# Block sums made in PSUM, a new order of block products and other pages for copies, in the middle stage of an attention and mixture-of-experts kernel

## The chip, the cores and the metric

The kernel runs on one core of a Trainium2 chip. The metric is the device time of one execution in microseconds (us). The engines are TensorE (PE, matmuls), VectorE (DVE), ScalarE (ACT), GpSimd (POOL), and SyncE (SP), whose queue issues most of the DMAs.

## The reference

`x` is the output of an attention block (a local window plus a downsampled part), 2304 tokens by 512. All numbers are fp32. Behind it stands a layer of eight experts, and it is there that the change lies:

```
P = exp(logits - logits.max())          # then normalised eight times by rows and columns
out = np.zeros((N, D), dtype=np.float32)
for e in range(E):                      # E = 8, D = 512, F = 1024
    h = np.maximum(x @ w1[e], 0.0)
    ye = h @ w2[e]
    out += P[:, e:e + 1] * ye
```

## The kernel before, in words

**Precision.** Every fp32 operand of a matmul is split into a high part (fp32r, made by ACT with a copy) and a low part (the rest, made by DVE or POOL with a subtraction). A product takes three matmuls: high by high, high by low, low by high.

**Stages.** The attention and the first experts come first (up to about 668 us). In the *middle stage* (class `Mid`, `final_plan(form="X")`, 668 to 914 us) three experts are computed for 1024 tokens by a fast block product: seven products of blocks instead of eight, for the price of sums of blocks before and after. A short *plain part* (`plain_part`, L2599 on, 914 to 953 us) follows: eight steps of ordinary products (`mm1` L2312, `mm2` L2331 to L2333), during which the operands of the last stage are prepared. The *last stage* (class `Final`, form "Y") does all eight experts for the last 1024 tokens, again with seven products, and keeps PE busy to the end.

**A round of the middle stage.** There are six rounds s (three experts, two halves of F each). A round has first-layer products `a1`..`a7` and `b1`..`b7` (the letter is the half of the columns of F) and second-layer products `1`..`7` that use the round before. A first-layer product is 6 matmuls of 512 columns (L573), a second-layer product 4 tiles of 6 matmuls of 256 columns (L755). The order on PE is written out by hand in strings: `PROX` for the first round, `MIDX` for the five next ones, `TAILX` for what is left of the second layer at the end.

The first-layer products go to two PSUM banks of a side, A (products 1, 6, 7, 4, summed in this order) and D (2, 5, 3). Between them ACT copies the bank to SBUF (`s1` after 1, `u2` after 6, `u3` after 7), and DVE forms sums: `c11` after 2, `c22` after 5 and 7, `c12` after 3. `c11` starts as bank D plus `s1`, and the bank is then started anew by product 5. When all seven are there, four more sums of relus are made (`S1` to `S4`). The function `hl` splits each result: `hi` on ACT, `lo` on DVE. The sums c11, c21, S1, S2, S3, S4, c12 are the operands of products 2, 1, 5, 6, 7, 3, 4 of the second layer. The results of the second layer are multiplied by the gate and added to accumulators by DVE (L766).

**Who sets the order.** `Plan.schedule` gives each operation a due time, counted back from PE's order, and writes every engine's queue in an order that follows from it. Pages of SBUF come from pools; `Mid.make` (L689 on) says which ring of values lies where: `five` are the eight pages of tile x5, `wb` and `ct` are pools with 8 and 4 pages. `self.five[6]` and `[7]` are free for sums or copies because the weights of layer one use six.

**Around the end of the middle stage.** The operands x4 and x5 of the last stage had been stored to `xc` in DRAM. `reload` (L2790) brings back two of the four slices of four tiles: the first half is issued behind the last first-layer product, the second half behind everything. `soon` (L2798) starts the weights of the plain part. In `plain_part`, `next(tg)` draws five operations at a time (`per`) from `t_gen` (L2620 on): sums of blocks of x4 and x5 (`bsum`, DVE L2627), split into `th` (ACT L2644) and `tl` (DVE). Their four buffers in pool `ct` are then taken by the gates `g` of the last stage (DMA L562).

Of the kernel before, what the change touches and what calls it, by code (L numbers as in the profile page):

```python
# [8 lines left out]
F32 = mybir.dt.float32  # L9
# [157 lines left out]

PRO = "a1 a2 f a6 a5 f b1 b2 a7 f f a4 f a3 b6 f b5 b7 f b4 b3 f".split()
MID = "1 a1 a2 2 a6 a5 5 a7 b1 6 a4 a3 3 b2 b6 7 b5 b7 4 b4 b3".split()
MIDX = "2 a1 a2 1 a6 a5 5 a7 b1 6 a4 a3 3 b2 b6 7 b5 b7 4 b4 b3".split()  # L170
PROX = "a1 a2 f a6 a5 f b1 b2 a7 f f a4 f a3 b6 f b5 b7 f b4 b3 f".split()
TAILX = "2 1 6 5 7 3 4".split()
MIDL = "1 a1 a2 2 a6 a5 5 a7 b1 6 a4 b2 3 a3 b6 b5 b7 7 b4 b3 4".split()
TAIL = "1 2 5 6 x11 7 3 x22 4 x12 4 x21".split()

# [1 line left out]
def final_plan(  # L177
# [3 lines left out]
    P = Plan()  # L181

    def E(f, *a):
        return lambda: getattr(em, f)(*a)
# [63 lines left out]
    def l1(s, p, i, conv, st):  # L248
        k = f"{p}{s}"
# [20 lines left out]
        if form == "X":  # L270
            if i == 2:
                m = st["m11"] = new(f"m11{p}")
                P.dve(f"c11 {k}", [bk, st["s1"]], [m], E("add", m, bk, st["s1"]))
                hl("c11", m, True, False, True)
            if i in (5, 7) and 5 in st and 7 in st:
                m = st["m22"] = new(f"m22{p}")
                P.dve(f"c22 {k}", [st[5], st["u3"]], [m], E("add", m, st[5], st["u3"]))
                P.act(f"r22 {k}", [m], [m], E("relu", m, m))
            if i == 3:
                P.dve(f"c12 {k}", [bk, st["u2"]], [bk], E("add", bk, bk, st["u2"]))  # L280
                hl("c12", bk, False, True, True)
            if i == 4:
                hl("c21", bk, False, True, True)
            if all(z in st for z in range(1, 8)):
                A, D, m11, m22, ms = st[4], st[3], st["m11"], st["m22"], new("ms")
                P.dve(f"S1 {k}", [D, m22], [ms], E("rcomb", ms, D, m22, False))
                P.dve(f"S3 {k}", [A, m22], [m22], E("rcomb", m22, A, m22, True))
                P.dve(f"S2 {k}", [A, ms], [A], E("rcomb", A, A, ms, True))
                hl("S1", ms, True, False)
                hl("S2", A, False, True)  # L290
                hl("S3", m22, True, False)
                P.dve(f"S4 {k}", [m11, A], [m11], E("rcomb", m11, m11, A, False))
                hl("S4", m11, True, False)
            return
        if i == 2:
            m = st["m11"] = new("m11" if masters == 2 else f"m11{p}")
# [351 lines left out]
class Mid(Final):  # L648
# [25 lines left out]
        self.first_r2 = 5 * len(es) * 2 % 6  # L674

    def page(self, home, z, dt=F32R):
        k = z in ("h", 0)
        if home in ("wa", "wb"):
            return self.take(home, "w1h" if k else "w1l", dt, "hx")
        if home == "hp":  # L680
            return self.take("hp", "hh" if k else "hl", dt, "hx")
        if home == "ct":
            return self.take("ct", "s", dt, "hx")
        if home == "four":
            return self.four[7]
        return self.rest.pop(0)

    def make(self, ring, i):
        if ring == "o1":  # L689
            t = self.four[i].rearrange("p (a c) -> p a c", a=4)  # L690
            return {"h": t[:, 0:2], "l": t[:, 2:4]}
        if ring == "o2":
            return {z: self.take("wa", "w2" + z, F32R, "o2").rearrange("p (a c) -> p a c", a=2) for z in "hl"}
        if ring in ("r1", "m11b", "m22b"):
            if not self.five:
                for z in "hl":
                    t = self.xq.tile([128, 4, 512], F32, name=f"x{z}5")
                    self.five += [t[:, k] for k in range(4)]
            return self.five[{"m11b": 6, "m22b": 7}.get(ring, i)]
        if ring == "r2":  # L700
            for n in (0, 3, 5, 4, 2, 1):
                self.made["r2", (self.first_r2 + n) % 6] = self.take("rawp", "r", F32, "r2")
            return self.made[ring, i]
        if ring == "ms":
            return self.take("ct", "s", F32, ring)
        if ring in ("s13", "u2", "m11a", "m22a"):
            return self.page("wb", int(ring in ("u2", "m22a")), F32)
        if ring[0] == "h":
            x, p = ring[1:-1], ring[-1]
            return {z: self.page(self.home[x, p, z], z) for z in "hl"}  # L710
        pool, tag = {"A": ("ps_h", "h"), "D": ("ps_a", "a"), "Y": ("ps_y", "y"), "Z": ("ps_z", "y")}[ring[0]]
        return self.take(pool, tag, F32, "psm")
# [62 lines left out]
def attention_moe_kernel(  # L775
# [1577 lines left out]
    with tc.manual_schedule():  # L2353
# [189 lines left out]
        new = []  # L2543
# [164 lines left out]
        def plain_part(rest, n0, limit, tg, ahead, held, h_next=None):  # L2708

            steps = [(p, e, f, n0 + i * NF + f) for i, (p, e) in enumerate(rest) for f in range(NF)]  # L2710
            per = -(-24 // max(1, len(steps) - 3))
            for si, (piece, e, f, n) in enumerate(steps):
                h_cur = mm1(piece, n) if h_next is None else h_next
                if si == 0:
                    while part1:
                        plain2()
                h_next = mm1(steps[si + 1][0], steps[si + 1][3]) if si + 1 < len(steps) else None
                if f == 0:
                    ye = [y_tile([128, DM], "psy") for _ in piece_tiles(piece)]
                pump(clk["pe"], clk["pe"] - 0.15)  # L2720
                if si >= len(steps) - 2:
                    held.append((
                        lambda t, h=h_cur, n=n, f=f, y=ye: mm2(h, n, y[t:t + 1], f, t),
                        lambda t, e=e, y=ye, l=piece_tiles(piece): combine(*l[t], e, y[t], accp),
                    ))
                else:
                    t2 = mm2(h_cur, n, ye, f)
                if f == NF - 1 and si < len(steps) - 2:
                    for (c, t), y in zip(piece_tiles(piece), ye):
                        combine(c, t, e, y, accp)  # L2730
                        dve(512, t2)
                while n_cv[0] < min(n + 5, limit):
                    w_convert(nc.vector)
                for _ in range(per if si >= 2 else 0):
                    next(tg, None)
                pump(clk["pe"], clk["pe"] - 0.15)
                ahead(si - len(steps))
# [59 lines left out]
        def soon():  # L2797
            for _ in range(2 * NRAW - 1):  # L2798
                raw_next()
            for _ in plain1():  # L2800
                pass

        then = {
            id([o for o in plan.seq if o.name == f"2t0 {ns - 1}"][0]): raw_next,
            id([o for o in plan.seq if o.name[0] in "ab"][-1]): lambda: reload(slice(0, 4, 2)),
            id([o for o in work if o.name.startswith("w2l")][-1]): soon,
        }
        for o in work:
            if o not in first:
                o.emit()  # L2810
            then.get(id(o), lambda: None)()
        reload(slice(1, 4, 2))
        for c, t in closing:
            closed(c, t, accp)
        final = Final(
# [58 lines left out]
```

## Time and profile before

| | us |
|---|---|
| median of 3 runs (1593.80 to 1597.13) | 1594.59 |
| the profiled execution: time | 1595.28 |
| the profiled execution: span on the core | 1593.5 |
| PE busy | 1569.8 (99%) |
| DVE busy | 1364.5 (86%) |
| POOL busy | 1080.3 (68%) |
| ACT busy | 810.7 (51%) |

The span runs from the first instruction to the last; 1.78 us of the execution lie around it. PE is busy nearly all the time, so what can be had are its idle stretches and those in which its clock is lower. These stand at the end of the slices 24 and 25 of 40 (956 to 1012 us), which are the end of the plain part and the beginning of the last stage; there are small ones in the middle stage.

### The profile page before, as it was taken

What the parts mean: (1) busy time and instruction counts of PE and PEld (TensorE: products, weight loads), DVE (VectorE), ACT (ScalarE), POOL (GpSimd) and SP (SyncE); (2) the same over time, 40 slices, a digit from 0 to 9 for tenths busy, and PEclk for the clock granted to TensorE, in tenths of its full rate; (3) what the DMA queues carried; (4) which work ended last, traced back from release to release, by engine and by line L of the source; (5) the groups of instructions that cost most, each with busy time, mean ns of one, the idle gap of its engine ahead of it and who ended that gap; (6) DMA issues with size and microseconds to landing.
All of it is one profiled execution on the core that took longest, in us unless ns stands there. A gap on an engine that the chain in (4) does not pass through costs nothing.

```text
span 1593.5 us, 24471 instructions
## 1 busy us (share of the span) xinstructions
PE 1569.8 (99%) x8220; PEld 1324.4 (83%) x8220; DVE 1364.5 (86%) x1878; ACT 810.7 (51%) x1739; POOL 1080.3 (68%) x998
## 2 busy tenths in 40 slices
PE   9999999999999999999999997999999999999998
PEld 7888888888888888888988986788888888888887
DVE  8678998778988587389999867899999999999987
ACT  4554555565455443354555344555555555555553
POOL 6688656868585500378888557777777777777772
PEclk9999999999999999999999998999999999999999
DMA  7878766868584645423331363222221222222101
GB/s 201 214 204 210 168 171 176 209 179 225 147 222 117 182 150 169 140 75 90 111 99 48 118 207 80 65 62 65 61 67 56 74 57 69 66 77 55 47 14 53
DMA packets 230701, 191.23 MB, mean 120 GB/s; under 512 B 26479, under 2 KB 188463, under 8 KB 230575
## 3 DMA queue, kind: packets, MB, share of 16 engines
q1 hardware_dynamic: 223470, 177.87, 41.2%
q10 hardware_dynamic: 7104, 11.80, 2.0%
q8 instruction: 64, 1.05, 0.3%
q14 instruction: 63, 0.51, 0.1%
HBM read 167.42 MB, written 22.18 MB: 119 GB/s over the span
## 4 chain that ended last, share of the span: by engine, by line
PE 83%; DVE 7%; DMA 3%; POOL 3%; issue 2%; ACT 1%; SPq 1%; ACTq 0%; POOLq 0%; DVEq 0%
PE psm L573 22%; PE psm L586 19%; PE psh L2072 17%; PE psy L2106 6%; PE psy L2107 5%; PE psy L2108 5%; PE psm L755 4%; DVE acc L766 2%; DVE acc L2597 1%; DVE hx L733 1%; POOL o L556 1%; PE pss L1697 1%; DMA r<-in_moe_w_dram 1%; DMA xl<-xc 1%; PE psg L1877 1%
## 5 line engine op out<-in xcount | busy, mean ns | idle before, releaser
L556 POOL TENSOR_TENSOR o<-r,o 128x512 fp32r<-128x512 f32 x126 | 169.2, 1343 | 68.9 <-ACT o L552 66.5
L2228 POOL TENSOR_TENSOR w1l<-r,w1h 128x512 fp32r<-128x512 f32 x112 | 156.6, 1398 | 85.0 <-ACT w1h L2205 78.0
L573 PE MATMUL psm<-th,o 128*128 128x512 f32 x512 | 174.6, 392 | 7.0 <-DVE s L602 4.7
L2228 POOL TENSOR_TENSOR w2l<-r,w2h 128x512 fp32r<-128x512 f32 x114 | 159.3, 1397 | 28.7 <-ACT w2h L2205 28.4
L2106 PE MATMUL psy<-w2h,hh 128*128 128x512 f32 x408 | 166.0, 407 | 0.0
L2107 PE MATMUL psy<-w2l,hh 128*128 128x512 f32 x408 | 159.9, 392 | 0.0
L2108 PE MATMUL psy<-w2h,hl 128*128 128x512 f32 x408 | 159.8, 392 | 0.0
L586 PE MATMUL psm<-hx,o 128*128 128x512 f32 (+1 forms) x588 | 155.2, 387 | 0.0
L556 POOL TENSOR_TENSOR o<-xh,o 128x256 fp32r<-128x256 f32 x132 | 110.9, 842 | 62.5 <-ACT o L552 61.9
L596 DVE TENSOR_TENSOR acc<-psm,acc 128x512 f32<-128x512 f32 x214 | 143.1, 679 | 7.7 <-PE psm L586 7.5
L2136 ACT ACTIVATE hh<-psh 128x512 fp32r<-128x512 f32 (+1 forms) x136 | 67.5, 496 | 161.0 <-PE psh L2072 151.5
L2139 DVE SCALAR_TENSOR_TENSOR hl<-psh,hh 128x512 fp32r<-128x512 f32 (+1 forms) x136 | 76.2, 560 | 76.4 <-ACT hh L2136 76.2
L573 PE MATMUL psm<-xh,o 128*128 128x512 f32 x384 | 132.0, 392 | 2.9 <-DVE hx L611 1.9
L2205 ACT ACTIVATE w2h<-r 128x512 fp32r<-128x512 f32 x133 | 83.7, 629 | 90.4 <-PE psy L2108 27.6
L586 PEld LDWEIGHTS psm<-hx,o 128*128 128x128 f32 x588 | 109.4, 189 | 22.2
L2072 PE MATMUL psh<-xhs,w1h 128*128 128x256 f32 (+1 forms) x384 | 125.1, 326 | 0.3 <-ACT xhs L1838 0.3
L2072 PE MATMUL psh<-xhs,w1l 128*128 128x256 f32 (+1 forms) x384 | 122.9, 320 | 1.2 <-DVE w1l L2224 1.2
L2072 PE MATMUL psh<-xls,w1h 128*128 128x256 f32 (+1 forms) x384 | 122.8, 320 | 0.2
L573 PEld LDWEIGHTS psm<-th,o 128*128 128x128 f32 x512 | 96.7, 189 | 28.2 <-DVE s L602 5.2
L556 POOL TENSOR_TENSOR xh<-xh,xh 128x256 fp32r<-128x256 f32 x32 | 27.5, 867 | 123.2 <-ACT xh L552 123.1
L1283 DVE TENSOR_REDUCE lo<-prod 128x256 f32<-128x1792 f32 x32 | 109.5, 3422 | 0.4
L552 ACT ACTIVATE o<-r 128x512 fp32r<-128x512 f32 x139 | 86.6, 626 | 41.1 <-PE psm L586 19.9
(349 smaller groups left out, 4590.4 us busy)
## 6 DMA issues: line engine op xcount, KB each, us to landing
r<-in_moe_w_dram SPq DMA_DIRECT2D x367, 256.0 KB
xh<-in_moe_w_dram SPq DMA_DIRECT2D x108, 128.0 KB
spill<-sp ACTq DMA_DIRECT2D x40, 256.0 KB
s<-spill SPq DMA_DIRECT2D x40, 256.0 KB
xl<-in_moe_w_dram SPq DMA_DIRECT2D x68, 128.0 KB
g<-gd SPq DMA_DIRECT2D x16, 256.0 KB
sums<-dr SPq DMA_DIRECT2D x36, 64.0 KB
r2x<-in_moe_w_dram SPq DMA_DIRECT2D x9, 256.0 KB
```

Of the source, the lines that this page charges most:

```text
L552: self.nc.scalar.activation(out=self.get(v)["h"], in_=self.w_view(l, r, ps), func=AF.Copy)
L556: (self.nc.gpsimd if pool else self.nc.vector).tensor_tensor(out=o["l"], in0=self.w_view(l, r, ps), in1=o["h"].bitcast(F32), op=ALU.subtract)
L573: self.nc.tensor.matmul(out=ps, lhsT=wt[:, k], rhs=xt[:, k], start=start and n == 0, stop=n == 5, skip_group_check=not start,)
L586: self.nc.tensor.matmul(out=ps, lhsT=wt[:, a, 128 * m:128 * m + 128], rhs=ht if part is None else self.cut(ht, part), start=start and n == ...
L596: self.nc.vector.tensor_tensor(out=self.get(o[0]), in0=self.get(a[0]), in1=self.get(b[0]), op=op)
L1283: nc.vector.tensor_reduce(out=ot[:, :, h % 2], in_=pr.rearrange("p r w d -> p r d w"), axis=AX.X, op=ALU.add,)
L2072: nc.tensor.matmul(out=ps, lhsT=w[:, kk], rhs=x[:, kk], start=(kk == 0 and j == 0), stop=(kk == 3 and j == 2),)
L2106: nc.tensor.matmul(out=ye[z], lhsT=hh[:, ts], rhs=h2, start=(f2 == 0), stop=False)
L2107: nc.tensor.matmul(out=ye[z], lhsT=hh[:, ts], rhs=l2, start=False, stop=False)
L2108: nc.tensor.matmul(out=ye[z], lhsT=hl[:, ts], rhs=h2, start=False, stop=(f2 == NF - 1))
L2205: nc.scalar.activation(out=h, in_=r, func=AF.Copy)
L2228: nc.gpsimd.tensor_tensor(out=l, in0=r, in1=h.bitcast(F32), op=ALU.subtract)
```

## The change

- `c11` is written back into bank D instead of an SBUF page. `hi` and `lo` read it there, with the relu in them as before. A new ACT operation (L737 after the change, 12 of them) writes relu(c11) to the page `m11`, which `S4` needs later.
- `S1`, `S2` and `S4` are written into bank D one after another, and `S3` into bank A; before, S1, S3 and S4 went to SBUF pages. A new ACT copy (12 of them) puts S1 on the page `ms`, which S2 needs. So all `lo` of these sums now read PSUM.
- The second-layer order becomes 2 1 5 6 7 4 3 (before 2 1 5 6 3 7 4 in the rounds and 2 1 6 5 7 3 4 at the end), and at the end of a round b3 stands ahead of b4.
- Pages: the copies s1, u2, u3 lie on pages 6 and 7 of x5, the masters `m11` and `m22` of both sides in `wb`. The pages of the second layer's weights are handed on in another order.
- The second half of `reload` is issued at the end of `soon`, which now comes behind the last low part of a second-layer weight or the last round's product 2, tile 3, whichever is later. On SP's queue the DMAs keep their sequence.
- `t_gen` is drawn from step 1 of the plain part instead of step 2.

```diff
-MIDX = "2 a1 a2 1 a6 a5 5 a7 b1 6 a4 a3 3 b2 b6 7 b5 b7 4 b4 b3".split()
+MIDX = "2 a1 a2 1 a6 a5 5 a7 b1 6 a4 a3 7 b2 b6 4 b5 b7 3 b3 b4".split()
-TAILX = "2 1 6 5 7 3 4".split()
+TAILX = "2 1 5 6 7 4 3".split()
             if i == 2:
                 m = st["m11"] = new(f"m11{p}")
-                P.dve(f"c11 {k}", [bk, st["s1"]], [m], E("add", m, bk, st["s1"]))
-                hl("c11", m, True, False, True)
+                P.dve(f"c11 {k}", [bk, st["s1"]], [bk], E("add", bk, bk, st["s1"]))
+                hl("c11", bk, False, True, True)
+                P.act(f"m11 {k}", [bk], [m], E("relu", m, bk), ps=True)
...
-                A, D, m11, m22, ms = st[4], st[3], st["m11"], st["m22"], new("ms")
-                P.dve(f"S1 {k}", [D, m22], [ms], E("rcomb", ms, D, m22, False))
-                P.dve(f"S3 {k}", [A, m22], [m22], E("rcomb", m22, A, m22, True))
-                P.dve(f"S2 {k}", [A, ms], [A], E("rcomb", A, A, ms, True))
-                hl("S1", ms, True, False)
-                hl("S2", A, False, True)
-                hl("S3", m22, True, False)
-                P.dve(f"S4 {k}", [m11, A], [m11], E("rcomb", m11, m11, A, False))
-                hl("S4", m11, True, False)
+                A, D, m11, m22 = st[4], st[3], st["m11"], st["m22"]
+                ms = new("ms")
+                P.dve(f"S1 {k}", [D, m22], [D], E("rcomb", D, D, m22, False))
+                P.act(f"ms {k}", [D], [ms], E("copy", ms, D), ps=True)
+                hl("S1", D, False, True)
+                P.dve(f"S2 {k}", [A, ms], [D], E("rcomb", D, A, ms, True))
+                hl("S2", D, False, True)
+                P.dve(f"S3 {k}", [A, m22], [A], E("rcomb", A, A, m22, True))
+                hl("S3", A, False, True)
+                P.dve(f"S4 {k}", [m11, D], [D], E("rcomb", D, m11, D, False))
+                hl("S4", D, False, True)
...
-        if ring in ("r1", "m11b", "m22b"):
+        if ring in ("r1", "s13", "u2"):
...
-            return self.five[{"m11b": 6, "m22b": 7}.get(ring, i)]
+            return self.five[{"s13": 6, "u2": 7}.get(ring, i)]
         if ring == "r2":
-            for n in (0, 3, 5, 4, 2, 1):
+            for n in (0, 5, 3, 4, 1, 2):
...
-        if ring in ("s13", "u2", "m11a", "m22a"):
-            return self.page("wb", int(ring in ("u2", "m22a")), F32)
+        if ring[0] == "m":
+            return self.page("wb", "hl"[ring[1] == "2"], F32)
...
-                for _ in range(per if si >= 2 else 0):
+                for _ in range(per if si >= 1 else 0):
                     next(tg, None)
...
             for _ in plain1():
                 pass
+            reload(slice(1, 4, 2))
...
-            id([o for o in work if o.name.startswith("w2l")][-1]): soon,
+            id([o for o in work if o.name.startswith(("w2l", f"2t3 {ns - 1}"))][-1]): soon,
...
             then.get(id(o), lambda: None)()
-        reload(slice(1, 4, 2))
```

DVE's queue in the plain part, before. `w2l` is the low part of a weight, `hl` that of the plain part's hidden layer, `bsum` and `tl` come from `t_gen`:

```order
L1010 TENSOR_TENSOR w2l<-r_10230,w2h 128x512
L2321 SCALAR_TENSOR_TENSOR hl<-psh,hh 128x512
L1010 TENSOR_TENSOR w2l<-r_10275,w2h 128x512
L2627 TENSOR_TENSOR bsum<-xh_9928,xl_9929 128x512
L2627 TENSOR_TENSOR bsum<-xh_628,xl_629 128x512
L2627 TENSOR_TENSOR bsum<-xh_9928,xl_9929 128x512
L2627 TENSOR_TENSOR bsum<-xh_628,xl_629 128x512
L2627 TENSOR_TENSOR bsum<-bsum 128x512
L2321 SCALAR_TENSOR_TENSOR hl<-psh,hh 128x512
```

The same place now:

```order
L1011 TENSOR_TENSOR w2l<-r_10254,w2h 128x512
L2628 TENSOR_TENSOR bsum<-xh_9947,xl_9948 128x512
L2628 TENSOR_TENSOR bsum<-xh_628,xl_629 128x512
L2628 TENSOR_TENSOR bsum<-xh_9947,xl_9948 128x512
L2628 TENSOR_TENSOR bsum<-xh_628,xl_629 128x512
L2628 TENSOR_TENSOR bsum<-bsum 128x512
L2322 SCALAR_TENSOR_TENSOR hl<-psh,hh 128x512
L1011 TENSOR_TENSOR w2l<-r_10299,w2h 128x512
```

The first five operations of `t_gen` moved ahead of one `hl` and one `w2l`; each later group of them moved ahead of one `hl` in the same way, up to the last four `tl`, behind which an `hl` now stands.

DVE's queue at the end of the third round, before, from the results of product 7 (L766 of acc_0_6927 to acc_3_6952) to `c22` of side b (L596, which writes page xl_7540):

```order
L766 SCALAR_TENSOR_TENSOR acc_3_6952<-psm,lg,acc_3_6952 128x256
L2597 SCALAR_TENSOR_TENSOR acc_1_7500<-s_8432,lg,acc_1_7500 128x512
L2597 SCALAR_TENSOR_TENSOR acc_0_7142<-s_8480,lg,acc_0_7142 128x512
L733 TENSOR_TENSOR hx<-ms,hx 128x512
L596 TENSOR_TENSOR xl_7540<-psm,hx 128x512
```

Now, from the results of product 4 to the same `c22` (L599, which writes a page of `wb`, shown as hx):

```order
L767 SCALAR_TENSOR_TENSOR acc_3_6952<-psm,lg,acc_3_6952 128x256
L730 SCALAR_TENSOR_TENSOR xhs<-psm,xhs 128x2x256
L740 SCALAR_TENSOR_TENSOR psm<-psm,hx 128x512
L2598 SCALAR_TENSOR_TENSOR acc_0_7142<-s_8554,lg,acc_0_7142 128x512
L734 TENSOR_TENSOR hx<-psm,hx 128x512
L599 TENSOR_TENSOR hx<-psm,xl_7540 128x512
```

The `lo` of S1 (L733 before, L734 now) reads `psm`, a bank, where it read the page `ms`; S1 itself (L740, psm to psm) stands in this stretch too; two additions of spilled results (L2597) became one.

ACT's queue in the same round now, from `hi` of c11 of side b to `hi` of S1 of side a and its copy:

```order
L723 ACTIVATE hx<-psm 128x512
L737 ACTIVATE hx<-psm 128x512
L596 ACTIVATE xl_7540<-psm 128x512
L555 ACTIVATE xh_628<-xh_7539 128x256
L723 ACTIVATE xhs<-psm 128x2x256
L555 ACTIVATE o_7883<-r_7553 128x512
L555 ACTIVATE xh_628<-xh_7539 128x256
L723 ACTIVATE hx<-psm 128x512
L596 ACTIVATE ms<-psm 128x512
```

L737 with psm behind it and the copy to `ms` are the new operations. DVE's `lo` of c11 and of S1 wait for both readings of the bank by ACT.

## Rows read from the trace of the kernel before

**Rows 1.** Windows: bounds, us, busy PE, PEld, DVE, ACT, POOL; PE clock, DMA, GB/s.

```profile
700.00:800.00 100.00, 99.56 (x639) 90.01 (x638) 98.26 (x156) 50.48 (x107) 81.56 (x74) 1.00 0.37 104
...
1100.00:1200.00 100.00, 100.00 (x443) 82.84 (x442) 94.60 (x136) 55.02 (x114) 77.92 (x79) 1.00 0.23 64
```

**Rows 2.** Windows of 10 us, PE alone: us, busy (x), clock, DMA share, GB/s.

```profile
960.00:970.00 10.00, 5.30 (x14) 0.53 0.56 134
```

**Rows 3.** Timeline of PE, 958 to 1007 us: start us, us, instruction, [idle before <-releaser].

```profile
958.89 0.50 PE L573 MATMUL psm<-th,o 128*128 128x512 f32 x1 [2.17 <-ACT s L593]
...
965.54 0.80 PE L573 MATMUL psm<-th,o 128*128 128x512 f32 x1 [4.70 <-DVE s L602]
...
971.10 0.39 PE L573 MATMUL psm<-xl,o 128*128 128x512 f32 x1
...
987.48 0.50 PE L573 MATMUL psm<-xh,o 128*128 128x512 f32 x1 [1.07 <-DVE xl L596]
...
1006.95 0.50 PE L573 MATMUL psm<-xh,o 128*128 128x512 f32 x1 [1.85 <-DVE hx L611]
```

**Rows 4.** Timeline of DVE, 931 to 965 us.

```profile
931.63 1.42 DVE L1010 TENSOR_TENSOR w2l<-r,w2h 128x512 fp32r<-128x512 f32 x1
...
944.29 0.68 DVE L2321 SCALAR_TENSOR_TENSOR hl<-psh,hh 128x512 fp32r<-128x512 f32 x1
...
951.68 0.69 DVE L2321 SCALAR_TENSOR_TENSOR hl<-psh,hh 128x512 fp32r<-128x512 f32 x1 [0.42 <-ACT hh L2318]
...
953.02 4.66 DVE L2627 TENSOR_TENSOR bsum<-bsum 128x512 f32<-128x512 f32 x4
...
958.21 4.10 DVE L2627 TENSOR_TENSOR tl<-bsum,th 128x512 fp32r<-128x512 f32 x4
...
964.79 0.69 DVE L602 SCALAR_TENSOR_TENSOR s<-psm,g 128x512 f32<-128x512 f32 x1 [1.87 <-DMA g<-gd]
```

**Rows 5.** Timeline of ACT, 956 us.

```profile
956.58 1.77 ACT L2644 ACTIVATE th<-bsum 128x512 fp32r<-128x512 f32 x3 [1.67 <-DVE bsum L2627]
```

**Rows 6.** Timeline of SP's queue, 906 to 959 us.

```profile
906.92 0.52 SPq L2795 DMA_DIRECT2D xl<-xc  x1
...
958.91 1.51 SPq L562 DMA_DIRECT2D g<-gd  x2
```

**Rows 7.** Timeline of PE, its waits in the middle stage.

```profile
690.62 0.50 PE L573 MATMUL psm<-th,xl 128*128 128x512 f32 x1 [1.18 <-ACT hx L593]
...
732.70 0.50 PE L573 MATMUL psm<-xh,xl 128*128 128x512 f32 x1 [0.41 <-DVE xl L596]
...
812.99 0.50 PE L573 MATMUL psm<-xh,xl 128*128 128x512 f32 x1 [0.69 <-DVE xl L596]
...
866.38 2.66 PE L755 MATMUL psm<-o,hx 128*128 128x256 f32 x20 [0.66 <-DVE hx L733]
```

**Rows 8.** Groups of DVE, 694 to 894 us: instruction xcount | busy us, mean ns.

```profile
L733 DVE TENSOR_TENSOR hx<-xl,hx 128x512 fp32r<-128x512 f32 x10 | 13.7, 1381 | 0.0
...
L733 DVE TENSOR_TENSOR hx<-ms,hx 128x512 fp32r<-128x512 f32 x10 | 12.9, 1290 | 0.0
...
L733 DVE TENSOR_TENSOR hx<-hx 128x512 fp32r<-128x512 f32 x12 | 11.9, 1000 | 0.0
...
L733 DVE TENSOR_TENSOR xls<-psm,xls 128x512 fp32r<-128x512 f32 x5 | 3.4, 681 | 0.1
```

**Rows 9.** Timeline of PE, 800 to 811 us.

```profile
800.90 0.39 PE L573 MATMUL psm<-th,xh 128*128 128x512 f32 x1
...
807.88 0.52 PE L755 MATMUL psm<-o,xhs 128*128 128x256 f32 x3
...
810.75 0.40 PE L573 MATMUL psm<-th,xl 128*128 128x512 f32 x1
```

**Rows 10.** Timeline of DVE, 803 to 813 us.

```profile
803.84 0.69 DVE L596 TENSOR_TENSOR xl<-psm,hx 128x512 f32<-128x512 f32 x1
...
812.26 0.68 DVE L596 TENSOR_TENSOR xl<-psm,hx 128x512 f32<-128x512 f32 x1
```

More of the change, by code (lines that the diff above doesn't have):

```diff
@@ L676, in page @@
     def page(self, home, z, dt=F32R):
-        k = z in ("h", 0)
+        k = z == "h"
         if home in ("wa", "wb"):
@@ L683, in page @@
             return self.take("ct", "s", dt, "hx")
-        if home == "four":
-            return self.four[7]
-        return self.rest.pop(0)
+        return self.rest.pop(0) if home == "rest" else self.four[7]
     def make(self, ring, i):
```

## The prediction

> **What bounds the kernel now.** I read the windows of 100 us first. In the middle stage PE is 99.56 us of 100 busy and DVE 98.26; in the last stage PE is 100.00 busy at a clock of 1.00 [rows 1]. The reader should see two things: PE sets the time everywhere, and DVE is nearly as full beside it, so any late DVE result shows as idle PE. In the last stage 443 matmuls of 512 columns take 100 us, 0.226 us each: that is the price of a matmul at full clock.
>
> A change that adds and removes no matmul can therefore only win or lose (a) idle PE and (b) PE at a lower clock. So next I looked for both in windows of 10 us and PE's timeline. From 960 to 970 us PE did 14 matmuls, and the granted clock was 0.53, about the lower of its levels, 1.2 GHz of 2.4 [rows 2]. The timeline around it shows 2.17 us of idle before 958.89, 4.70 before 965.54, then thirteen matmuls from 965.54 to 971.10 (5.56 us, at full clock 13 x 0.226 = 2.94, so 2.6 lost), and two later waits of 1.07 and 1.85 [rows 3]. The engine had idled 6.87 of the 8.8 us before 965.54, with one group of matmuls between; the clock was back by 971.
>
> Who was late? DVE's timeline says it: five sums (one at 952.29, L2627, behind the `hl` of 951.68; four from 953.02 for 4.66 us), one `hl`, four `tl` from 958.21, then r11 (L602) at 964.79, which had waited 1.87 us for the DMA of the gate g [rows 4]. The third `th` on ACT ends at 956.58 + 1.77 = 958.35; the copy of a6's bank stands behind it, and PE gets it at 958.89 [rows 5]. SP issues the first g at 958.91, since g takes a buffer that the first `tl` frees [rows 6]. So one chain, last sums, `tl`, g, r11, a5, ends both large waits.
>
> In the middle stage the waits are single: 1.18, 0.41, 0.69 and 0.66 us, 2.94 in all [rows 7]. Two are on L596 of DVE (c22), one on `lo` (L733), one on ACT.
>
> **Part 1: `t_gen` a step earlier.** Nothing is added; the same 24 operations stand one step (5.44 us of the plain part) further ahead in DVE's queue. The last five sums now stand behind the `hl` of 944.29 rather than that of 951.68. That `hl` ends at 944.97. Five sums of 4.66/4 = 1.17 us give 944.97 + 5.83 = 950.8. Behind them one `hl` stays, which cannot start before 951.68 (it waited for ACT's `hh`, 0.42 us of idle before it) and ends at 952.37 [rows 4]. So the four `tl` start at 951.4 to 952.4 instead of 958.21. From there the old distances hold: g 0.70 later, r11 5.88 later (964.79 - 958.91), a5 0.75 later: a5 could start at 958.7 to 959.7 instead of 965.54. The three `th` no longer stand ahead of a6's copy, so a6 starts 2.17 earlier, at 956.72, and its six matmuls end at 958.1 (six of 0.226; 958.7 if some run at the lower clock). a5 then waits 0 to 1.6 us; I take 1.0. The gain is 2.17 + 4.70 - 1.0 = **5.9 us**. With no long idle stretch the clock has no cause to fall by what the trace shows here: **2.6 us** more. The 1.07 and 1.85 stand behind other sums of the new round; I leave both.
>
> What is moved has its price. The `hl` of the plain part come behind five sums, up to 5.8 us later. Each is needed by mm2 one step later; steps are 5.44 us and the `hl` stands a first-layer product ahead of its use, so I take 0, and up to 1 us if one is late. The sums read slices of x4 and x5: SP's fourth issue of the first half came at 906.92, held by the last reader of m22b [rows 6]; now only copies lie there, so that it, the weights and the output stores behind it come some us earlier. No PE idle of over 0.2 us lies in 914 to 956 us, so an earlier transfer is worth 0 there, and no price either unless its traffic delays a weight.
>
> **Part 2: sums in PSUM.** The groups of DVE from 694 to 894 us show 32 `lo` (10 + 10 + 12) that read SBUF and take 1381, 1290 and 1000 ns, 38.5 us together; the five `lo` that read a PSUM bank take 681 ns [rows 8]. At 681 the 32 cost 21.8. So DVE loses 16.7 us per 200, from some 98% busy to about 90%. Beside it the Trainium skill's page "Perfetto Trace Analysis", section "Optimizing Scalar/DVE Operations", speaks against the change: it gives DVE about 60 ns of access overhead on SBUF and about 125 on PSUM. By it the 48 `lo` of all six rounds would cost 48 x 65 ns = 3.1 us more instead of less (an estimate from that page); the rows differ from it in sign, since here the neighbour's load on SBUF seems to cost more than the bank does.
>
> ACT gets 24 operations. No row shows relu(c11) or a copy of S1 from a bank; `th` takes 1.77/3 = 0.59 each. 14 us on an engine that is 50% busy lie beside other work. But a chain gets longer: bank D is free for product 5 only after c11 (0.69), `hi`, the new reading (0.59 each) and `lo` (0.68), 2.55 us, where c11 alone freed it before. The room is what PE does in between: a second-layer block, 807.88 to 810.75, 2.87 us, and a product of six matmuls, 1.36: 4.23 [rows 9]. So the chain fits where c11 starts up to 1.68 us after its product's end; only in the first round, where a5 has 2.04 us of room, I charge 0.6. How late c11 starts now is seen at 803.84, 2.94 us after b2 (six matmuls before 800.90) gave its bank [rows 10], but that is with a full DVE queue.
>
> **Part 3: the order.** b3 now follows the block right behind b7, so c22 has 2.87 us instead of 4.23. Before, c22 of that round began at 812.26 and ended at 812.94, against a block that ended at 810.75. With the old lag that is a wait of 2.19 us. With DVE 16.7 us emptier, and one addition fewer ahead of it in that queue, I take it that c22 ends within the block in most rounds. The 2.94 us of old waits go but for the 0.6 and some 0.3 of small ones: **2.0 us**. The bounds are a gain of 2.94 and the losses in the rivals.
>
> **The sum.** 5.9 + 2.6 + 2.0 = 10.5 us. The profiled execution took 1595.28 (span 1593.5, 1.78 around it), so 1584.8; it lies 0.69 above the median of the runs shown, so 1584.1.
>
> **Rivals.**
> 1. *b3 waits for c22.* Two rounds with the old waits plus the lost 1.36 (1.77 and 2.05) and three with 0 to 1.36 each, 2.0 together: 5.8 instead of 2.94 in the middle stage. 1595.28 - 8.5 + 2.9 = 1589.7, by the median 1589.0. For: c22 depends on DVE's lag, which [rows 10] show. Against: the emptier queue. 0.13.
> 2. *The change at the transition does not do what it says*: a5 waits for something else just as late (a weight, a conversion on POOL, the SP queue), so only the 2.0 come: 1592.6. Against: a5's wait ends with r11 and g, and both hang on `tl`. 0.07.
> 3. *All idle stretches go*, the 1.07 and 1.85 too: 2.94 + 2.17 + 4.70 + 2.6 + 2.92 = 15.3, so 1579.3. 0.07.
> 4. *PSUM reads cost DVE more.* If `lo` from PSUM were 65 ns dearer and all of it reached PE: 1595.28 - 8.5 + 3.1 = 1589.9, by the median 1589.2. It is the rule of the page above; 681 against 1000 ns and more speak against it. 0.03.
> 5. *Slower: bank D becomes the bound.* If DVE's lag stays as at 803.84, the chain is 2.94 + 2.55 = 5.49 against 4.23 of room, 1.26 us of wait each for a5 and b5, and b3 waits 2.19: 4.7 per round, 23.6 in five. 1595.28 - 8.5 + 23.6 = 1610.4, by the median 1609.7. It turns slower where the waits pass 1.7 us a round. Against: the lag comes from the queue that gets 16.7 us per 200 shorter. 0.06.
>
> **How the numbers follow.** Forecast 0.64, the rivals 0.13, 0.07, 0.07, 0.03 and 0.06. The range 1578.0 to 1591.5 holds the forecast and rivals 1, 3 and 4, some 0.85. A measurement can tell 0.2% (3.2 us) from no change, so faster is below 1591.4: forecast, rivals 1, 3 and 4, less 0.04 for their tails, 0.83; same 0.07 + 0.04 = 0.11; slower 0.06.
>
> **What would show it.** Right: `tl` at 951 to 953, g some 0.7 us behind, a5 before 960, no window of clock 0.53 near 960; the `lo` groups (L734) at about 0.68 us, and DVE under 92% from 700 to 800. Wrong: waits of 1 us or more before b3 on c22, or before a5 and b5 on the `lo` of c11, in each round (rivals 1 and 5); a5 near 965 (rival 2); PE idle in 914 to 956 us, behind a late `hl`.

## The result, and the profile after

The change took 1581.6 us (median of 4 runs, 1580.12 to 1583.35) against 1594.26 for the kernel before (1593.80 to 1597.13): a ratio of 0.9917, with a 95% interval of 0.9900 to 0.9934. That is 12.7 us less; 10.5 less had been forecast. The profiled execution took 1583.35 us with a span of 1581.6, which is 11.9 less than the span of before.

PE's timeline gives the same program points in both kernels: the first matmul of the middle stage, of the plain part, of a5, and the b1 that [rows 3] show behind the 1.85 us wait. The differences of their starts say where the time went:

| stretch, us | before | after | difference |
|---|---|---|---|
| middle stage | 246.47 | 243.95 | -2.52 |
| plain part up to a5 | 50.98 | 44.09 | -6.89 |
| a5 to that b1 | 41.41 | 38.93 | -2.48 |
| that b1 to the end | 586.54 | 586.27 | -0.27 |

(The start of the middle stage lies 0.22 us later after the change; with it the differences make 11.94. In all fourteen profiles of this document that start lies between 666.55 and 668.67 us, so a difference of the times can hold up to 2 us that no edit made.) The windows of the profile after, with the columns of [rows 1], answer to [rows 1, 2]:

```profile
700.00:800.00 100.00, 100.00 (x644) 91.36 (x643) 90.87 (x161) 58.13 (x119) 80.74 (x80) 1.00 0.39 118
...
960.00:970.00 10.00, 10.00 (x46) 8.29 (x45) 7.87 (x10) 5.71 (x12) 8.06 (x9) 1.00 0.40 112
```

PE idles no more from 700 to 800 us, DVE is busy 90.87 us there where it was 98.26, and from 960 to 970 PE does 46 matmuls at a clock of 1.00 where it did 14 at 0.53. Behind that stand PE's waits, as its timeline has them; these are all of 0.2 us and over from 668 to 1060 us:

```profile
673.90 0.50 PE L576 MATMUL psm<-th,xh 128*128 128x512 f32 x1 [0.67 <-DVE hx L730]
...
903.15 3.13 PE L756 MATMUL psm<-o,hx 128*128 128x256 f32 x24 [0.51 <-DVE acc L767]
...
956.35 0.50 PE L576 MATMUL psm<-th,o 128*128 128x512 f32 x1 [0.90 <-DVE s L605]
...
975.81 0.50 PE L576 MATMUL psm<-xh,o 128*128 128x512 f32 x1 [1.06 <-DVE xl L599]
...
995.28 0.70 PE L576 MATMUL psm<-xh,o 128*128 128x512 f32 x1 [1.87 <-DVE hx L614]
```

Of [rows 3], the waits of 2.17 and 4.70 have become one of 0.90 (a5, 956.35), and 1.07 and 1.85 are still there. Of the four in [rows 7] none is left; new are 0.67 in the first round (a5, behind the `lo` of c11) and 0.51 in the last blocks of the second layer. DVE's timeline of after shows the chain to a5:

```profile
927.57 2.49 DVE L2628 TENSOR_TENSOR bsum<-xh,xl 128x512 f32<-128x512 f32 x4
...
942.61 5.23 DVE L2628 TENSOR_TENSOR bsum<-bsum 128x512 f32<-128x512 f32 x4
...
948.26 0.69 DVE L2322 SCALAR_TENSOR_TENSOR hl<-psh,hh 128x512 fp32r<-128x512 f32 x1 [0.42 <-ACT hh L2319]
948.87 4.26 DVE L2628 TENSOR_TENSOR tl<-bsum,th 128x512 fp32r<-128x512 f32 x4
...
955.60 0.69 DVE L605 SCALAR_TENSOR_TENSOR s<-psm,g 128x512 f32<-128x512 f32 x1 [1.26 <-DMA g<-gd]
```

and SP's queue of after the reload's fourth transfer and the first g:

```profile
892.53 0.55 SPq L2796 DMA_DIRECT2D xl<-xc  x1
...
949.72 1.52 SPq L565 DMA_DIRECT2D g<-gd  x2
```

The last four sums begin at 942.61 instead of 953.02; the `hl` of 948.26 stands in front of the `tl`, held by ACT as in [rows 4]; g goes out 0.85 us behind the first `tl`, r11 comes 5.88 behind g, and a5 0.75 behind r11. The reload's fourth transfer, at 906.92 in [rows 6], went out at 892.53. And the group of DVE from 694 to 894 us that answers to [rows 8]:

```profile
L734 DVE TENSOR_TENSOR hx<-psm,hx 128x512 fp32r<-128x512 f32 x31 | 21.2, 684 | 2.7 <-ACT ms L596 2.7
```

The `lo` that took 1000 to 1381 ns from SBUF take 684 from a bank.

### The profile page after: what moved, and what is told of

Read it like the earlier page. It is cut to its first block, busy times and chain, and to the rows that moved or that the text cites. A ratio compares the mean times of both kernels' runs of the same rounds, so it can differ in the third digit from the quotient of the medians.

```text
span 1581.6 us, 24565 instructions
## 1 busy us (share of the span) xinstructions
PE 1565.8 (99%) x8220; PEld 1322.6 (84%) x8220; DVE 1342.5 (85%) x1878; ACT 825.0 (52%) x1763; POOL 1068.8 (68%) x998
## 4 chain that ended last, share of the span: by engine, by line
PE 91%; DVE 4%; DMA 1%; issue 1%; SPq 1%; ACT 1%; POOL 1%; ACTq 0%; DVEq 0%; POOLq 0%
PE psm L576 25%; PE psm L589 19%; PE psh L2073 18%; PE psm L756 7%; PE psy L2107 6%; PE psy L2108 6%; PE psy L2109 6%; PE pss L1698 1%; PE psh L2313 1%; PE psg L1878 1%; SPq L1067 1%; PE psx L1822 0%; DVE acc L767 0%; PE psd L1760 0%; PE psd L1731 0%
## 5 line engine op out<-in xcount | busy, mean ns | idle before, releaser
L599 DVE TENSOR_TENSOR acc<-psm,acc 128x512 f32<-128x512 f32 x214 | 143.3, 680 | 7.9 <-PE psm L589 7.8
L559 POOL TENSOR_TENSOR o<-xl,o 128x256 fp32r<-128x256 f32 x92 | 76.3, 831 | 42.1 <-ACT o L555 42.1
```

The lines of the kernel that those rows point to most:

```text
L559: (self.nc.gpsimd if pool else self.nc.vector).tensor_tensor(out=o["l"], in0=self.w_view(l, r, ps), in1=o["h"].bitcast(F32), op=ALU.subtract)
L599: self.nc.vector.tensor_tensor(out=self.get(o[0]), in0=self.get(a[0]), in1=self.get(b[0]), op=op)
```

## Experiments

All ratios are to the kernel before, run on the same chip beside them; brackets hold the 95% interval. Names that begin with b_ are edits of the kernel before, a_ of the kernel after, and c_ of a_c11sbuf. Stretches are those of the table above.

### Does the earlier step alone bring the transition's gain?

b_step1 and a_step2 change one line, in opposite directions:

```diff
-                for _ in range(per if si >= 2 else 0):
+                for _ in range(per if si >= 1 else 0):
```

> The kernel before, with only the drawing of t_gen moved to step 1 of the plain part. Theory (the transition's gain is the chain last sums, tl, g, r11, a5, and owes nothing to the sums in PSUM): the middle stage keeps its idle of about 2.9 us, a6 starts without a wait, a5 waits 0.5 to 1.5 us, the clock stays at 1.00 behind it; about 9.4 us less than before, 1585. Rival (the sums need the earlier pages: the fourth transfer of the reload still waits for the last reader of m22b): the first sum waits for its slice, a5 waits over 3 us, the clock drops again, 1588 to 1594.

> The kernel after, with t_gen drawn from step 2 as before. Theory (two independent gains): the middle stage stays 2.5 us shorter than before, the waits of 2.2 and 4.7 us and the stretch at the lower clock come back; 1591 to 1592. Rival (the emptier DVE queue is what brings the tl early): the waits come back only in part, under 1588.

b_step1: 1588.95 us, 0.9968 [0.9956, 0.9980]. a_step2: 1591.07, 0.9977 [0.9968, 0.9986]. a_step2 came as the theory said: a middle stage of 243.99, waits of 2.17 and 4.88 us, a5 50.86 us behind the plain part's start. b_step1 lay between theory and rival: 6.0 us less and not 9.4, a time in the rival's range, but with 1.99 us of wait before a5 and no stretch at the lower clock behind it. Its a5 came 48.18 us behind the plain part's start, against 44.09 after. PE's timeline in b_step1 shows waits that neither kernel has, for `hl`, and a longer one of a5:

```profile
938.34 0.50 PE L2333 MATMUL psy<-w2h,hl 128*128 128x512 f32 x1 [0.75 <-DVE hl L2321]
...
949.68 0.50 PE L2333 MATMUL psy<-w2h,hl 128*128 128x512 f32 x1 [0.17 <-DVE hl L2321]
...
955.55 0.50 PE L573 MATMUL psm<-xh,o 128*128 128x512 f32 x1 [0.54 <-DVE hl L2321]
...
962.63 0.50 PE L573 MATMUL psm<-th,o 128*128 128x512 f32 x1 [1.99 <-DVE s L602]
```

and DVE's timeline of it why:

```profile
928.50 0.94 DVE L1010 TENSOR_TENSOR w2l<-r,w2h 128x512 fp32r<-128x512 f32 x1 [7.06 <-ACT w2h L1007]
930.46 0.69 DVE L1010 TENSOR_TENSOR w2l<-r,w2h 128x512 fp32r<-128x512 f32 x1 [1.02 <-ACT w2h L1007]
931.11 0.69 DVE L2321 SCALAR_TENSOR_TENSOR hl<-psh,hh 128x512 fp32r<-128x512 f32 x1
932.15 1.43 DVE L1010 TENSOR_TENSOR w2l<-r,w2h 128x512 fp32r<-128x512 f32 x1 [0.35 <-ACT w2h L1007]
933.50 3.58 DVE L2627 TENSOR_TENSOR bsum<-xh,xl 128x512 f32<-128x512 f32 x4
```

DVE stands idle for 7.06 us before the first low part of a weight (928.50); before the change it was 6.38 us (to 927.93), and no PE wait came of it. Three of them crowd in behind one another, and the first sum begins only at 933.50, 19.05 us behind the plain part's start; after the change it is 15.31 (927.57). What is late are the weights, which stand on SP's queue behind the reload's fourth transfer. The low part of 928.50 belongs to the weight issued at 923.77, which stands behind that transfer (906.82), six weights, the second half of the reload and the output stores (914.04 to 923.04). That queue in b_step1:

```profile
906.82 0.52 SPq L2795 DMA_DIRECT2D xl<-xc  x1
...
907.39 0.60 SPq L976 DMA_DIRECT2D r<-in_moe_w_dram  x1
...
923.14 0.53 SPq L976 DMA_DIRECT2D r<-in_moe_w_dram  x1
923.77 0.50 SPq L981 DMA_DIRECT2D r<-in_moe_w_dram  x1
```

So the pages were exchanged too, and nothing else:

```diff
-        if ring in ("r1", "m11b", "m22b"):
+        if ring in ("r1", "s13", "u2"):
...
-            return self.five[{"m11b": 6, "m22b": 7}.get(ring, i)]
+            return self.five[{"s13": 6, "u2": 7}.get(ring, i)]
...
-        if ring in ("s13", "u2", "m11a", "m22a"):
-            return self.page("wb", int(ring in ("u2", "m22a")), F32)
+        if ring in ("m11a", "m22a", "m11b", "m22b"):
+            return self.page("wb", int(ring[1] == "2"), F32)
```

> The kernel before with t_gen from step 1, and the pages of the copies and the masters exchanged as in the change; sums and orders as before. Theory (in b_step1 the sums stood behind low parts of weights that came late, because the reload's fourth transfer, at 907 us, held SP's queue; with the pages exchanged it goes out before 897 and everything behind it too): the first sum begins 3 to 4 us sooner after the start of the plain part than the 19.0 us of b_step1, the wait of 0.75 us for hl goes, a5 waits at most 1.2 us; some 4 us less than b_step1, 1584.5 to 1586. Rival (the SP queue is held by something else, or only the shorter middle stage brings the loads early): as b_step1, 1589.

1583.46 us, 0.9938 [0.9925, 0.9952]: 10.3 us less than before where b_step1 had 6.0. By the stretches it is 8.8 (6.35 up to a5 and 2.47 from there to that b1) where b_step1 has 5.3 (2.80 and 2.48), so the 9.4 of the theory of b_step1 are nearly reached. The first sum begins 15.73 us behind the plain part's start, the waits for `hl` are gone, and a5 waits 1.42, a little over the 1.2 expected. The weight that went out at 923.77 goes out at 919.57. The fourth transfer on its SP queue:

```profile
894.40 0.52 SPq L2795 DMA_DIRECT2D xl<-xc  x1
```

and the first sums on its DVE:

```profile
928.98 2.48 DVE L2627 TENSOR_TENSOR bsum<-xh,xl 128x512 f32<-128x512 f32 x4
```

The other way round, a_pages is the kernel after with the pages as before:

```diff
-        if ring in ("r1", "s13", "u2"):
+        if ring in ("r1", "m11b", "m22b"):
...
-            return self.five[{"s13": 6, "u2": 7}.get(ring, i)]
+            return self.five[{"m11b": 6, "m22b": 7}.get(ring, i)]
...
-        if ring[0] == "m":
-            return self.page("wb", "hl"[ring[1] == "2"], F32)
+        if ring in ("s13", "u2", "m11a", "m22a"):
+            return self.page("wb", "hl"[ring in ("u2", "m22a")], F32)
```

> The kernel after with the copies in pool wb and the masters of side b on pages 6 and 7 of x5, as before. Theory (the pages let the reload, and the weights behind it on SP's queue, go out early, and t_gen from step 1 needs that): SP issues the reload's third or fourth transfer 8 us or more later than after's 892 us, a5 waits 1.5 to 4 us in place of 0.9, the middle stage stays 2.5 us shorter than before; 1583.5 to 1586. Rival (with the sums in PSUM the last readers are early anyway): as after, 1581 to 1582.5.

1589.98 us, 0.9973 [0.9964, 0.9983]: 4.9 us less than before instead of 12.7, and lost in another place than expected. The fourth transfer did go out late (902.90, behind S4, which reads `m11` of side b and ends at 902.83), but a5 waited 0.99 as after; the time was lost before the plain part, whose start came 8.2 us later against the middle stage's. The wait in a_pages on PE's timeline:

```profile
913.51 1.01 PE L756 MATMUL psm<-o,xhs 128*128 128x256 f32 x3 [6.27 <-DVE acc L767]
```

and what stands behind it on ACT's:

```profile
907.79 0.63 ACT L2657 ACTIVATE w1h<-r 128x512 fp32r<-128x512 f32 x1 [7.74 <-DMA r<-in_moe_w_dram]
909.66 0.63 ACT L2657 ACTIVATE w1h<-r 128x512 fp32r<-128x512 f32 x1 [1.24 <-DMA r<-in_moe_w_dram]
911.22 0.63 ACT L2657 ACTIVATE w1h<-r 128x512 fp32r<-128x512 f32 x1 [0.94 <-DMA r<-in_moe_w_dram]
911.76 0.58 ACT L723 ACTIVATE hx<-psm 128x512 fp32r<-128x512 f32 x1
```

On ACT, the `hi` of the last S4 (911.76) stands behind three high parts of weights (L2657) that wait for their DMAs; the `lo` waits for that `hi`, an addition stands behind the `lo` on DVE, and PE waits 6.27 us for it; most of the rest of the 8.2 is the lower clock behind that wait (the blocks from 913.51 on). In the kernel after, the last of the three ends at 903.89, the `hi` starts at 903.79, and PE doesn't wait at that place. So the early pages are worth 4 to 8 us, at one of two places: the sums of the plain part, or S4. No run exchanges the pages alone, with the old sums and `t_gen` from step 2.

### Sums and order, apart

b_sums is the kernel after with these four lines as before:

```diff
-MIDX = "2 a1 a2 1 a6 a5 5 a7 b1 6 a4 a3 7 b2 b6 4 b5 b7 3 b3 b4".split()
+MIDX = "2 a1 a2 1 a6 a5 5 a7 b1 6 a4 a3 3 b2 b6 7 b5 b7 4 b4 b3".split()
-TAILX = "2 1 5 6 7 4 3".split()
+TAILX = "2 1 6 5 7 3 4".split()
...
-            for n in (0, 5, 3, 4, 1, 2):
+            for n in (0, 3, 5, 4, 2, 1):
...
-                for _ in range(per if si >= 1 else 0):
+                for _ in range(per if si >= 2 else 0):
```

b_mid is the kernel before with the first and the third of them as after:

```diff
-MIDX = "2 a1 a2 1 a6 a5 5 a7 b1 6 a4 a3 3 b2 b6 7 b5 b7 4 b4 b3".split()
+MIDX = "2 a1 a2 1 a6 a5 5 a7 b1 6 a4 a3 7 b2 b6 4 b5 b7 3 b3 b4".split()
...
-            for n in (0, 3, 5, 4, 2, 1):
+            for n in (0, 5, 3, 4, 1, 2):
```

> The kernel after with both order strings and the order of the weights' pages as before, and t_gen from step 2: the sums in PSUM and the pages alone. Theory (the middle stage gains by the emptier DVE queue): its idle of 2.9 us falls to between 0.5 and 1.2, only the first round's a5 waits some 0.6; DVE 90 to 92 us busy of 100 from 700 to 800; about 1592. Rival (the gain comes from the new order): idle of 2.5 us or more, 1594.

> The kernel before with the new order in the rounds (b3 behind the block that follows b7) and the pages of the weights that go with it; sums still in SBUF. Theory (b3 has 1.36 us less room, and DVE's lag is the old one): b3 waits for c22 1.8 and 2.2 us in two rounds and up to 1.4 in the others; idle of the middle stage 5 to 8 us, 1596 to 1600. Rival (two additions of DVE trade places with the order, so c22 comes earlier by itself): idle under 3 us, 1592 to 1594.5.

b_sums: 1611.3 us, 1.0104 [1.0090, 1.0117]. Theory and rival both failed: it is 16 us slower, and the middle stage lasts 262.54 us. b_mid: 1593.94, 0.9994 [0.9986, 1.0003], no difference; its middle stage lasts 246.10 and has the 1.18 us of before and waits of 1.19 and 0.38 for c22, 2.75 in all. The 5 to 8 of the theory did not come; the rival held. In b_sums the last blocks of the second layer, whose order was put back too, wait 2.01 and 0.68 us, and the first product of each of four rounds waits 2.4 to 3.0 us, with the lower clock behind three of these waits. Before the first of them, on ACT in b_sums:

```profile
730.43 0.60 ACT L723 ACTIVATE xhs<-psm 128x512 fp32r<-128x512 f32 x1 [0.47 <-PE psm L756]
```

on DVE:

```profile
732.25 0.68 DVE L730 SCALAR_TENSOR_TENSOR xhs<-psm,xhs 128x512 fp32r<-128x512 f32 x1
732.96 0.70 DVE L740 SCALAR_TENSOR_TENSOR psm<-psm,hx 128x512 f32<-128x512 f32 x1
...
738.67 0.68 DVE L734 TENSOR_TENSOR hx<-psm,hx 128x512 fp32r<-128x512 f32 x1
```

and on PE:

```profile
739.41 0.80 PE L576 MATMUL psm<-xhs,xh 128*128 128x512 f32 x1 [3.04 <-DVE hx L734]
```

At 730.43 ACT splits c12 (`hi`), and what it waited for is PE's L756, a second-layer block: the round before still used the page that c12 is split into, as the operand of block 4, and block 4 was the last block of the round, with only two first-layer products behind it. Then comes `lo` (732.25), and only then may S1 overwrite bank D (732.96). The chain of S1 to S4 comes behind it, each sum split before its bank is written again; the `lo` of S3 (738.67) ends at 739.35, and a1 of the next round, which waits for S3's bank A, starts at 739.41. Before the change, S1 went to a page, and PE has no wait at that place. Two kernels test it, each with another end of `MIDX` in the kernel after; the first piece is a_b4b3, the second a_swap34:

```diff
-MIDX = "2 a1 a2 1 a6 a5 5 a7 b1 6 a4 a3 7 b2 b6 4 b5 b7 3 b3 b4".split()
+MIDX = "2 a1 a2 1 a6 a5 5 a7 b1 6 a4 a3 7 b2 b6 4 b5 b7 3 b4 b3".split()
...
-MIDX = "2 a1 a2 1 a6 a5 5 a7 b1 6 a4 a3 7 b2 b6 4 b5 b7 3 b3 b4".split()
+MIDX = "2 a1 a2 1 a6 a5 5 a7 b1 6 a4 a3 7 b2 b6 3 b5 b7 4 b3 b4".split()
```

> The kernel after with b4 ahead of b3 again at the end of a round, block order 7 4 3 kept. Theory (what makes room for the sums in PSUM is block 4 ahead of 3, since it frees the page that c12 is split into, and c12 must be split before S1 may overwrite bank D): nearly as after, at most 1 us of idle per round more, 1581 to 1586. Rival (b3 early is what gives the chain of four sums its time): waits of 1.4 us or more before the next round's a1 or a2 in each round, 1589 or more.

> The kernel after with blocks 3 and 4 exchanged in the rounds (block 4 last again), b3 ahead of b4 kept. Theory (block 4's page): S1 of a side cannot be made before block 4 has ended, the chain S1, S2, S4 ends late, and the next round's first products wait 2 to 3 us in each of five rounds with a stretch at the lower clock behind it: 1592 to 1598. Rival (b3's place decides): as after, 1580 to 1584.

a_b4b3: 1585.61 us, 0.9949 [0.9936, 0.9961]. a_swap34: 1597.46, 1.0023 [1.0014, 1.0033]. With block 4 late the 2.4 us are back in four rounds and the middle stage lasts 261.36; with block 4 early and only b4 and b3 exchanged it lasts 247.58. There a5 waits 0.70 us for the `lo` of c11 in each of four more rounds. The first of these waits on PE in a_b4b3:

```profile
743.13 0.50 PE L576 MATMUL psm<-th,xh 128*128 128x512 f32 x1 [0.70 <-DVE hx L730]
```

and that before the next round in a_swap34:

```profile
737.49 0.50 PE L576 MATMUL psm<-xhs,xh 128*128 128x512 f32 x1 [2.38 <-DVE hx L734]
```

The theory of a_swap34 had five such rounds; four have it. So, by the middle stage, block 4's place is worth some 17 us to the sums in PSUM, b3's some 3.6; to the sums in SBUF the order is worth nothing that could be measured.

### The price of c11 in its bank, and what is left

a_c11sbuf is the kernel after with c11 on a page again; the other sums stay in PSUM:

```diff
-                P.dve(f"c11 {k}", [bk, st["s1"]], [bk], E("add", bk, bk, st["s1"]))
-                hl("c11", bk, False, True, True)
-                P.act(f"m11 {k}", [bk], [m], E("relu", m, bk), ps=True)
+                P.dve(f"c11 {k}", [bk, st["s1"]], [m], E("add", m, bk, st["s1"]))
+                hl("c11", m, True, False, True)
```

> The kernel after with c11 written to an SBUF page as before (12 ACT operations m11 fewer; bank D free right behind c11). Theory (the longer chain behind c11 costs only the 0.67 us that the first round's a5 waits, and DVE has room for lo from a page at 785 to 949 ns): that wait goes, no other comes, 0 to 1 us faster than after, 1580.5 to 1582. Rival (DVE's time counts): new waits on DVE of over 1 us in the middle stage, 1583 or more.

1581.66 us, 0.9925 [0.9911, 0.9938]; not to be told from after by its time. The 0.67 us wait is gone, one of 0.22 us at 689.78 is new, and the middle stage is 243.42, 0.53 us shorter. By that stretch c11 in its bank is a loss of half a microsecond in a change that is a gain; the time does not show it.

Two edits of it aim at the remaining waits, the first piece in c_step0, the second in c_fb3, and both in c_both:

```diff
-                for _ in range(per if si >= 1 else 0):
+                for _ in range(per):
...
-PRO = "a1 a2 f a6 a5 f b1 b2 a7 f f a4 f a3 b6 f b5 b7 f b4 b3 f".split()
+PRO = "a1 a2 f a6 a5 f b1 b2 a7 f f a4 f a3 b6 f b5 b7 f b4 f b3".split()
```

> a_c11sbuf with t_gen from step 0 of the plain part. Theory (a5's last 1.08 us of wait hang on the hl of the step before last, behind which the tl stand): the tl and g come another 5 us earlier, the wait goes, 1.1 us less than a_c11sbuf by the stage, 1580.5. Rival (what is moved up delays the low parts of the weights or an hl): idle of PE in the plain part of 0.5 us or more, no gain or a loss, 1581.5 to 1584.

> a_c11sbuf with the last held group of three matmuls ahead of b3 in the first round of the last stage (it stood behind it). Theory (b3 waits 1.07 us for c22, and three matmuls of 0.68 us can stand in that wait): the wait falls to about 0.4, 0.7 us less by the stage, 1581. Rival (the later end of that group delays its addition on DVE, and c22 or the next first layer with it): no gain.

> a_c11sbuf with both: t_gen from step 0 and the held group ahead of b3. Theory: the two add up, 1.8 us less than a_c11sbuf by the stages; 1580, 0.9910 to 0.9925 of the kernel before. Rival (one of them costs what the other brings): 1581.5 or more.

c_step0: 1580.45 us, 0.9910 [0.9896, 0.9923]. c_fb3: 1582.43, 0.9927 [0.9914, 0.9941]. c_both: 1580.7, 0.9911 [0.9897, 0.9924]. In c_step0 a5's wait is gone and 0.3 us before a1 of the last stage have come; a5 stands 43.54 us behind the plain part's start, 0.7 sooner than in a_c11sbuf. In c_fb3 the wait for c22 fell from 1.07 to 0.38, and 0.58 of a new one came behind it, as the rival had it (PE in c_fb3):

```profile
974.06 0.50 PE L575 MATMUL psm<-xh,o 128*128 128x512 f32 x1 [0.38 <-DVE xl L598]
...
987.65 0.50 PE L588 MATMUL psm<-xhs,o 128*128 128x512 f32 x1 [0.58 <-DVE o L558]
```

In c_both a5's wait is gone and the two others stand as in c_fb3 (0.37 and 0.59). From the middle stage's start to that b1 it takes 325.72 us, c_step0 325.71, c_fb3 326.53 and a_c11sbuf 326.61: the held group brings next to nothing, and the 1.8 us of the theory of c_both did not come.

c_step0 has the lowest time, and by its stretches it is 1.1 us better than after up to a5; by the intervals it isn't told apart from after.

## Why the prediction was right, and where it was not

The time lay in the range and on the forecast's side, 2.5 us below the number. Two of its reasons were incomplete all the same: it gave the pages nothing, and it did not say that the sums in PSUM need the order. The change holds all of these parts together, and so the number owes something to luck. By its steps:

- **What bounds the kernel**: right. The difference lies in PE's waits, in small losses of PE beside them, and in its stretch at the lower clock; no matmul was added (8220 in both profiles).
- **The chain to a5**: right in size. Forecast were a gain of 5.9 and a wait of 1.0; measured were 6.89 and 0.90. The wait itself and the 2.17 make 5.97 of it; the rest are small losses of before that no step had: 0.4 us in a6's six matmuls, whose starts lie 1.54 us apart (958.89 to 960.43, at a granted clock of 1.00) where five steps of 0.226 are 1.13, 0.3 us at 931 in the plain part, and some 0.2 beside the wait that is gone.
- **The lower clock**: 2.6 forecast, 2.48 measured. a_step2, b_sums and b_mid, with waits of over 4 us before a5, all have it again; b_step1 with 1.99 and b_step1_pages with 1.42 don't.
- **"An earlier transfer is worth 0 there"**: wrong. This is the step that failed. The page was misread too: the `lo` of S4 on `m11` of side b ends at 906.90 and the fourth transfer is issued at 906.92, so it waited for that page and not for m22b. PE's lack of idle in 914 to 956 us says that the transfers were early enough for the old order. With the sums a step earlier the weights' low parts stand right in front of them on DVE, and the transfers become what is late: b_step1 got 6.0 us, b_step1_pages 10.3. The waits for `hl` that the prediction named as a sign of failure came in b_step1, 1.46 us in all. What the prediction gave to the step alone belongs to the step and the pages together; whether the pages alone are worth something with the old order, no run shows.
- **DVE's relief**: right. 684 ns against a forecast of 681, DVE 90.87 busy against "about 90%". The Trainium skill's figures ("Perfetto Trace Analysis", "Optimizing Scalar/DVE Operations") would have DVE pay more for a bank than for SBUF; the measured pair here, 684 against 1000 to 1381 ns, goes the other way, so rival 4 falls. The trace of before also shows what the `lo` from SBUF paid for. Of its 36 `lo` with both operands in SBUF (L733, middle stage), the six that no POOL operation overlaps by the profile's spans take 0.67 to 0.69 us, the other 30 take 0.70 to 1.81. The 12 with one operand in a bank (L733) take 0.67 to 0.69 with POOL beside them or without, and so do all 48 after (L734, 0.68 to 0.69). Two of before that stand behind each other, while a POOL operation runs from 810.11 to 811.18:

```profile
810.51 1.23 DVE L733 TENSOR_TENSOR hx<-ms,hx 128x512 fp32r<-128x512 f32 x1
811.66 0.68 DVE L733 TENSOR_TENSOR hx<-hx 128x512 fp32r<-128x512 f32 x1
```

So a bank costs these operations no more than SBUF does, and what the change takes away is the delay beside POOL's work.

- **Middle stage**: 2.0 forecast, 2.52 measured, with the 0.6 for the first round's a5 found as 0.67. The waits alone fell by 1.76 (2.94 to 0.67 and 0.51); the rest are small losses beside them. That the shorter `lo` bring it was not shown by itself, since the sums in PSUM without the order lose more than that. The order was priced as a cost (b3 has less room for c22), and b_mid shows that cost to be none: c22 stands by its due time in DVE's queue, and when b3 moves forward, c22 does too. In b_mid it begins at 809.73, 2.38 us after b7 (block behind it from 807.35), where [rows 10] have 812.26, 4.38 after the block's start in [rows 9]. So rivals 1 and 5, built on DVE's old lag, had the wrong lag.
- **What no step and no rival named**: that the order carries the sums. The slower case was in reach, by a bank that is handed over too late, as rival 5 had it, and of its size (16 us in b_sums); but its seat was c12's page and block 4, not c11's chain.

The sizes add up within the intervals: pages and step 10.3 us (b_step1_pages), sums and order with the pages 3.9 (a_step2), 14.2 together, where both at once gave 12.7. By the stretches, which leave out the start and the end, it is 8.8 for the transition in b_step1_pages and 2.5 for the middle stage in a_step2, 11.3, where the change has 11.9.

## What to carry to other kernels

An operation made in place must wait for all that still reads the place, and those readers for their own pages; before one moves a result into a buffer that it shares, one follows the old content to its last reader's last page. A transfer that costs nothing now is not free for an order that asks for its data a step earlier: a moved consumer and the loads it needs are priced together. A part of a change that measures as nothing alone (the order, 0.9994) can be what keeps another from costing 16 us.

## What the runs showed that was not expected

The wait before b1 of the last stage's second round is 1.81 to 1.93 us long in all fourteen profiles, and PE does the same work around it. In seven of them the clock falls behind it and the next 8 us hold 1.7 to 1.8 us of loss (matmul starts against 0.227 us each); in the other seven it doesn't fall and the loss is 0.2 or less. Here the window from 994 to 998 us, of PE alone (us, busy, clock, DMA share, GB/s), in after:

```profile
994.00:998.00 4.00, 2.72 (x7) 0.68 0.40 112
```

and in a_c11sbuf:

```profile
994.00:998.00 4.00, 3.08 (x13) 1.00 0.42 127
```

The stretch from there to the end is 586.27 us in after and 584.61 in a_c11sbuf for the same instructions. The difference of 1.66 us is a good part of what the runs of one kernel lie apart; the four runs of after have mean clocks of 0.997 or 0.999. What decides it, no run here shows. Differences of under 2 us between medians were therefore read from the stretches before that point.
